# First expert's first weight block: loaded from GpSimd's queue in step 15, split in steps 18 and 19

## The chip, the cores and the metric

The kernel runs on one core of a Trainium2 chip. The metric is the device time of one execution in microseconds (us), as a median over runs. TensorE (PE), VectorE (DVE), ScalarE (ACT), GpSimd (POOL) and SyncE (SP) each work through an instruction stream of their own, in order. SP's stream holds almost only transfers (DMAs); GpSimd can issue transfers as well, on a queue of its own (q0 in the profile; SP's is q1).

## What is computed

Retention attention (4 batches, 8 heads, 768 positions, head size 64, blocks with a decayed state), and behind it a mixture of 8 experts, where each of the 3072 rows goes to the expert with the largest logit:

```python
x = attn_out.transpose(0, 2, 1, 3).reshape(3072, 512)
e_idx = np.argmax(x @ w_gate, axis=1)
for e in range(8):
    mask = e_idx == e
    h = np.maximum(x[mask] @ w1[e], 0.0)          # 512 -> 1024
    out[mask] = gate_w[mask, None] * eom[mask, e, None] * (h @ w2[e])   # 1024 -> 512
```

All in float32. The kernel gets that accuracy from fast products: each factor is split into a high part (a rounded copy) and a low part (the rest), and three products are summed (high by high, low by high, high by low).

## The kernel before

**Stages.** The attention is cut into 24 tiles of 128 rows, n = 0 to 23, six chunks of four batches. A software pipeline runs over steps s = -2 to 21. In step s, `stage_a(s+2)` turns keys and queries of tile s+2 on TensorE (`pk`, `pq`), and ScalarE copies them out (`kT`, `qT`); `stage_c1(s)` multiplies the decayed queries `qd` with the state (into `po`); `stage_b(s+1)` makes the scores (`ps`), which VectorE multiplies with the decay (`at`); `stage_c(s)` adds the scores' part to `po`, ScalarE copies it out as `xT`, and the state is updated from `pst`. Tiles 22 and 23 are finished by straight code behind the loop. GpSimd makes `qd` and `kd` (decayed queries and keys), scatters the routing records of the rows into a table in DRAM (`tab_d`), loads index lists from that table, and gathers rows of x (`xg`). From step 14 on the first expert is known, from the first 12 tiles; in step 15 its first index list is loaded (`load_rows(0, 0, 2, nc.gpsimd)`, called `index_0` below). The second index list is loaded behind the loop, when all earlier scatters have landed (`index_1` below).

**Weights.** Each expert's w1 and w2 come in two pieces of 1 MB each, `raw_i` (128 partitions, four runs of 512 numbers). Three buffers hold them. `load_piece(i)` issues the transfer; `split_hi(i, j)` is a ScalarE cast of a quarter into `whi`; `split_lo2(i, h)` is a VectorE subtraction over half a piece into `wlo` (raw minus `whi`, 128x1024). Before, `load_piece(0)` stood in step 18 (RES + 2, with RES = 16) on SP's queue, pieces 1 and 2 in steps 20 and 21. The four `split_hi(0, ...)` and two `split_lo2(0, ...)` stood behind the loop, between the last tiles. Piece 3 takes the buffer of piece 0 and waits until piece 0 is split.

**What sets the order.** The code stands in the order in which each engine runs it (`tc.manual_schedule()`); waits are added by the framework where an instruction needs another's result or buffer. `work` is a table of what is issued between the parts of a step, by engine GpSimd mostly. The first experts' products (`ph`, then `pyr`) begin as fillers between the last routing steps; behind them TensorE runs through all eight experts.

Of the kernel before, what the change touches and what calls it, by code (L numbers as in the profile page):

```python
# [23 lines left out]
def kernel(  # L24
# [13 lines left out]
    nc = tc.nc  # L38
# [37 lines left out]
    RES = 16  # L76
    RES0 = RES - B
# [23 lines left out]
    def turned_out(i):  # L101
        return pieces[i][1] == 1 and pieces[i][0] in TURNED

    def by_quarter(t):
        return t.rearrange("p (q d c) -> p q d c", q=4, d=4)

    def by_part(t):
        return t.rearrange("p (d q c) -> p q d c", q=4, d=4)

    def load_piece(i, eng=nc.sync, j=None):  # L110
        if i >= len(pieces):
            return
        p, m, s = pieces[i]
        src = (w1, w2)[m][bass.ds(expert[p], 1)]
        src = src[:, :, s * HALF : (s + 1) * HALF] if m == 0 else src[:, s * HALF : (s + 1) * HALF, :]
        if i not in raws:
            raws[i] = wpool.tile([P, 4, 512], F32, tag="raw", bufs=3, name=f"raw_{i}")
        c = slice(0, 4) if j is None else slice(j, j + 1)
        eng.dma_start(raws[i][:, c, :], src.rearrange("e (c p) f -> p (e c) f", p=P)[:, c, :])

    def split_hi(i, j):
        if i >= len(pieces):
            return
        if pieces[i] not in wparts:
            wparts[pieces[i]] = (
                wpool.tile([P, 4, 512], F32R, tag="whi", bufs=4, name=f"whi_{i}"),
                wpool.tile([P, 4, 512], F32R, tag="wlo", bufs=4, name=f"wlo_{i}"),
            )
        src, hi = raws[i][:, j, :], wparts[pieces[i]][0][:, j, :]
        if turned_out(i):  # L130
            src, hi = by_quarter(src), by_part(hi)
        nc.scalar.copy(out=hi, in_=src)  # L132
# [10 lines left out]
    def split_lo2(i, h):  # L143
        sl = slice(2 * h, 2 * h + 2)
        hi, lo = (t[:, sl, :] for t in wparts[pieces[i]])
        nc.vector.tensor_tensor(out=lo, in0=raws[i][:, sl, :], in1=hi.bitcast(F32), op=ALU.subtract)  # L146
# [149 lines left out]
    def blank_rows():  # L296
        norow = wpool.tile([P, E * EB * 3], I32, tag="raw", bufs=3, name="norow")
        nc.gpsimd.memset(norow, NOROW)
        nc.sync.dma_start(tab_d.rearrange("(p r) t -> p (r t)", p=P), norow)
# [132 lines left out]
    def stage_c(n):  # L432
        L = live[n]
        c, b = divmod(n, B)
        vt = qkv[n][2]
        xT = slot(f"xT_{n}")
        for y in range(2):
            po = L["po"][y]
            for m in range(4):
                i, j = divmod(m, 2)  # L440
                nc.tensor.matmul(  # L441
                    po[j * D : (j + 1) * D, i * P : (i + 1) * P],
                    vt[:, 4 * y + m, :],
                    L["at"][y][:, m, :],
                    start=(c == 0),
                    stop=(c == 0 or m >= 2),
                )
            nc.scalar.copy(out=xT[:, 256 * y : 256 * y + 256], in_=po[:, 0:256])
        L["xT"] = xTs[n] = xT
        if c < NCH - 1:  # L450
            pst = bank(f"pst_{n}")
            for m in range(4):
                for y in range(2):
                    nc.tensor.matmul(  # L454
                        pst[y * D : (y + 1) * D, m * D : (m + 1) * D],
                        L["kd"][:, 2 * m + y, :],
                        vt[:, 4 * y + m, :],
                        start=True,
                        stop=True,
                    )  # L460
            psv = pst[:, 0 : 4 * D].rearrange("p (m d) -> p m d", m=4)
            if c == 0:
                nc.vector.tensor_copy(out=state[b], in_=psv)
            else:
                for m in range(4):
                    nc.vector.scalar_tensor_tensor(
                        out=state[b][:, m], in0=state[b][:, m], scalar=qdec[:, m, P - 1 : P], in1=psv[:, m],
                        op0=ALU.mult, op1=ALU.add,
                    )
            weave()  # L470
            weave()
# [356 lines left out]
    def load_rows(p, j0=0, j1=None, eng=nc.sync):  # L828
        if p >= E:
            return  # L830
        n = (KT[p] if j1 is None else j1) - j0
        t = const.tile([32, 4, n, 3], I32, name=f"index_{p}_{j0}")
        src = tab_v[bass.ds(expert[p], 1)][:, :, j0 : j0 + n, :]
        eng.dma_start(t, src.rearrange("e (b r) j t -> (e r) b (j t)", b=4))
        idxs[(p, j0)] = (t, n)
# [381 lines left out]
    with tc.manual_schedule():  # L1217
# [15 lines left out]
        def rec():  # L1233
# [4 lines left out]
            RES0 - 1: ([], [rec], [rec]),  # L1238
            RES0: ([], [], []),
            RES0 + 2: ([], [rec], [rec]),  # L1240
            RES0 + 3: ([], [rec], [rec, lambda: load_rows(0, 0, 2, nc.gpsimd)]),
            RES + 2: ([row(2)], [], [row(3)]),
            RES + 3: ([row(4)], [], [row(5)]),
            RES + 4: ([rec], [], [rec]),
# [4 lines left out]
        for s in range(-2, NTILE - 2):  # L1249
            if s >= 0:  # L1250
                load_up_to(s + AHEAD - (4 <= s <= RES), 2 if s <= RES else 1)
            for i in range(3):
                if s == RES + (2, 4, 5)[i]:
                    load_piece(i)
            if s == -2:
                decay_table()
            if s == 0:
                stage_b(1)
                stage_b2(1)
            rest = stage_a(s + 2)  # L1260
            if late and s != RES + 5:
                late.pop(0)()
            if s >= 1 and s % B == 0:
                logits(s - B, B)
            for f in rest:
                f()
            if s >= 0:
                stage_c1(s)
            stage_a2(s + 2)
            if s == RES + 4:  # L1270
                stage_q(s + 2)
            if s + 1 >= 0 and s != 0:
                stage_b(s + 1)
            if s == RES + 5:
                late.pop(0)()
                seen = rank_counts("plater")
            n = s - 1
            if s >= 1 and s % B == 0:
                logit_rows(s - B)
            if n >= 0 and n % B == B - 1:  # L1280
                choice = route_choose(n + 1 - B, n + 1)
                ranking = route_place(n + 1 - B, n + 1)
                if s != RES + 4:
                    at_once(choice)
                    pace(uncounted[-1][0][0:1, 0, 0:1])
                per_turn[0] = 3 if n >= RES else 2
            if s == RES + 5:
                stage_d2(LAST)
            if s + 1 >= 0 and s != 0:
                stage_b2(s + 1)  # L1290
            stage_k(s + 2)
            if s == RES0 + 2:
                expert_regs(0, order_i, 1)
            if s == RES + 5:
                for f in held[:6]:
                    f()
                x_turn(0, 0)
            gap_work(s, "end")
            if s == RES + 4:
                at_once(choice[:-1])  # L1300
            if 0 <= n < LAST:
                stage_d2(n)
            if s == 0:
                later.extend(inter_tables())
                routing_tables()
                order_tables()
            if s == 1:
                weave(len(later))
            if s == 2:
                blank_rows()  # L1310
            if s >= 0:
                stage_c(s)
            if s == RES + 4:
                choice[-1]()
            if s == RES + 1:
                row_index(0)
                row(0)()
                row(1)()
            if ranking and s == RES + 4:
                late.append(ranking[0])  # L1320
                held = ranking[1:]
                ranking = []
            if ranking and s != RES0:
                late.append(ranking[0])
                later.extend(ranking[1:])
                ranking = []
            if ranking:
                for f in pick_first():
                    f()
                late.append(ranking[0])  # L1330
                later.extend(ranking[1:])
                ranking = []
            if s < RES0 - 2:
                place_scatter(1)

        n = NTILE - 1
        for j in range(2):
            split_hi(0, j)
        stage_c1(n - 1)
        stage_b(n)  # L1340
        stage_b2(n)
# [8 lines left out]
            x_hi(0, g, 0)  # L1350
        for g in range(NPAIR):
            x_lo(0, g, 0)
        split_lo2(0, 0)
        split_hi(0, 2)
        load_piece(3)
        stage_c1(n)
        stage_c(n)
        split_hi(0, 3)
        split_lo2(0, 1)
        for i in range(2):  # L1360
            rows_of(LAST + i)
        logits(LAST, B)
# [249 lines left out]
```

## Time and profile before

| what | value |
|---|---|
| median of three runs | 417.85 us (416.82 to 417.86) |
| the profiled execution, its own time | 415.14 us |
| its span, first to last instruction | 413.4 us |
| TensorE busy | 400.8 us (97%) |
| VectorE, ScalarE, GpSimd busy | 286.7, 190.4, 238.8 us |
| granted TensorE clock, mean | 0.998 |

The span ends with TensorE's last products and the scatter of the last rows. Shares of busy time are means over stages; a stage's own bound is read from what its instructions wait for, and an idle engine matters only where another engine waits for it.

### The profile page before, as it was taken

The numbers are of one execution on the slowest core, as the hardware profiler recorded it, in microseconds if no ns is written. First come the engines' busy times: TensorE is split into PE (matmuls) and PEld (weight loads), VectorE is DVE, ScalarE is ACT, GpSimd is POOL, SyncE is SP. The second block draws the span as 40 slices with busy tenths as digits, with TensorE's granted clock in tenths as the row PEclk, the third lists the DMA queues.
The fourth block names the chain that finished last, engine by engine and source line by source line (L and its number), as shares of the span: only waits on it lengthen the run. The fifth ranks groups of instructions, "written<-read, shape, count | busy, mean of one in ns | idle before, by whom it ended". The sixth has DMA issues, their size and how long they took to land.

```text
span 413.4 us, 10570 instructions
## 1 busy us (share of the span) xinstructions
PE 400.8 (97%) x3869; PEld 367.1 (89%) x3869; DVE 286.7 (69%) x810; ACT 190.4 (46%) x460; POOL 238.8 (58%) x301
## 2 busy tenths in 40 slices
PE   7999999999899999999999999999999999999994
PEld 4889878798698698999999999999999989989983
DVE  2759697877888646876868857957965864873710
ACT  4767665665684033544145325504704543542400
POOL 5367679668846788674783665467386266120012
PEclk9999999999999999999999999999999999999999
DMA  8999898889972764544479548746846884461001
GB/s 177 231 254 246 226 258 224 215 230 259 322 231 79 222 206 144 170 141 135 150 209 297 198 135 241 262 178 200 292 140 186 295 271 151 127 224 46 5 27 52
DMA packets 95103, 79.11 MB, mean 191 GB/s; under 512 B 58445, under 2 KB 70769, under 8 KB 95041
## 3 DMA queue, kind: packets, MB, share of 16 engines
q1 hardware_dynamic: 88080, 64.88, 53.2%
q0 software_dynamic: 6240, 12.93, 10.0%
q8 instruction: 32, 0.52, 0.5%
q10 hardware_dynamic: 720, 0.53, 0.5%
q14 instruction: 31, 0.25, 0.2%
HBM read 62.25 MB, written 16.45 MB: 190 GB/s over the span
## 4 chain that ended last, share of the span: by engine, by line
PE 85%; DVE 6%; DMA 5%; issue 2%; POOL 1%; ACT 0%; POOLq 0%; DVEq 0%; SPq 0%
PE ph_None L86 10%; PE ph_None L87 10%; PE ph_None L85 10%; PE py L87 6%; PE py L86 6%; PE py L85 6%; PE pyr L86 5%; PE pyr L87 5%; PE pyr L85 5%; PE ps L400 4%; PE po L441 4%; PE pk L341 3%; PE po L424 2%; PE pq L341 2%; DVE at L409 2%; PE pst L454 2%
## 5 line engine op out<-in xcount | busy, mean ns | idle before, releaser
L900 POOL DMA_INDIRECT xg<-x_d,rows x100 | 110.6, 1106 | 54.8 <-issue 28.9
L1009 ACT ACTIVATE hhi<-ph_None 128x400 fp32r<-128x400 f32 (+4 forms) x56 | 28.1, 501 | 115.8 <-PE ph_None L87 111.0
L86 PE MATMUL ph_None<-xlo,whi 128*128 128x400 f32 (+4 forms) x224 | 76.2, 340 | 0.0
L87 PE MATMUL ph_None<-xhi,wlo 128*128 128x400 f32 (+4 forms) x224 | 76.1, 340 | 0.0
L85 PE MATMUL ph_None<-xhi,whi 128*128 128x400 f32 (+4 forms) x224 | 76.1, 340 | 0.0
L132 ACT CAST whi<-raw 128x512 fp32r<-128x512 f32 x128 | 74.7, 615 | 2.4 <-DMA raw<-in_moe_w_dram 2.4
L141 DVE TENSOR_TENSOR wlo<-raw,whi 128x512 fp32r<-128x512 f32 x112 | 74.5, 686 | 0.7 <-ACT whi L132 0.5
L1010 DVE SCALAR_TENSOR_TENSOR hlo<-ph_None,hhi 128x400 fp32r<-128x400 f32 (+4 forms) x56 | 31.9, 570 | 35.2 <-ACT hhi L1009 33.2
L87 PE MATMUL py<-hhi,wlo 128*128 128x400 f32 (+2 forms) x128 | 44.4, 347 | 0.0
L86 PE MATMUL py<-hlo,whi 128*128 128x400 f32 (+2 forms) x128 | 44.4, 347 | 0.0
L85 PE MATMUL py<-hhi,whi 128*128 128x400 f32 (+2 forms) x128 | 44.4, 347 | 0.0
L86 PEld LDWEIGHTS ph_None<-xlo,whi 128*128 128x128 f32 x224 | 42.0, 188 | 0.5 <-DVE xlo L935 0.2
L1126 POOL DMA_INDIRECT out_dram<-yn,table x12 | 12.5, 1045 | 51.8 <-DVE yn L1190 34.6
L85 PEld LDWEIGHTS ph_None<-xhi,whi 128*128 128x128 f32 x224 | 42.0, 188 | 0.4
L87 PEld LDWEIGHTS ph_None<-xhi,wlo 128*128 128x128 f32 x224 | 42.0, 188 | 0.2
L345 ACT COPY qT<-pq 64x256 f32<-64x256 f32 x96 | 37.8, 393 | 2.0 <-PE pq L341 1.0
L409 DVE TENSOR_TENSOR at<-ps,decay 128x512 f32<-128x512 f32 x48 | 31.1, 681 | 10.4 <-PE ps L400 10.4
L86 PE MATMUL pyr<-wlo,hhi 128*128 128x512 f32 (+2 forms) x96 | 37.8, 394 | 0.5 <-DVE wlo L146 0.5
L87 PE MATMUL pyr<-whi,hlo 128*128 128x512 f32 (+2 forms) x96 | 37.6, 391 | 0.0
L85 PE MATMUL pyr<-whi,hhi 128*128 128x512 f32 (+2 forms) x96 | 37.5, 390 | 0.0
L931 ACT CAST xhi<-y 128x256 fp32r<-128x256 f32 (+3 forms) x64 | 19.5, 357 | 31.5 <-DVE y L917 31.5
L679 POOL DMA_INDIRECT tab_d<-rec,idx x24 | 26.2, 1090 | 10.0 <-issue 4.1
(216 smaller groups left out, 783.0 us busy)
## 6 DMA issues: line engine op xcount, KB each, us to landing
raw<-in_moe_w_dram SPq DMA_DIRECT2D x32, 1024.0 KB
x_d<-xn SPq DMA_DIRECT2D x22, 256.0 KB
qkv<-in_k_dram SPq DMA_DIRECT2D x40, 128.0 KB
qkv<-in_v_dram SPq DMA_DIRECT2D x20, 256.0 KB
qkv<-in_q_dram SPq DMA_DIRECT2D x36, 128.0 KB
yd<-yo SPq DMA_DIRECT2D x12, 256.0 KB
yr<-yd SPq DMA_DIRECT2D x48, 64.0 KB
xg<-x_d,rows POOLq DMA_INDIRECT x100
```

Of the source, the lines that this page charges most:

```text
L85: nc.tensor.matmul(ps, a[0], b[0], start=first, stop=False)
L86: nc.tensor.matmul(ps, a[0], b[1], start=False, stop=False)
L87: nc.tensor.matmul(ps, a[1], b[0], start=False, stop=last)
L132: nc.scalar.copy(out=hi, in_=src)
L141: eng.tensor_tensor(out=lo, in0=src, in1=hi.bitcast(F32), op=ALU.subtract)
L341: nc.tensor.transpose(out=dst[:, m * P : (m + 1) * P], in_=src[:, m], identity=ident)
L345: copies = [lambda r=r, view=view, src=src: nc.scalar.copy(out=view(qT[r]), in_=src) for r, view, src in query_parts(pq)]
L409: nc.vector.tensor_tensor(out=at, in0=ps.rearrange("p (g t) -> p g t", g=NPAIR), in1=dec[:, j], op=ALU.mult)
L679: nc.gpsimd.indirect_dma_start(out=tab_d, out_offset=bass.IndirectOffsetOnAxis(ap=idx, axis=0), in_=rec, in_offset=None, bounds_check=P * ...
L900: nc.gpsimd.indirect_dma_start(out=xg[(p, i)][:, m * P : (m + 1) * P], out_offset=None, in_=x_q[0 : 4 * rows], in_offset=bass.IndirectOffs ...
L1009: nc.scalar.activation(out=hi[:, r], in_=ph[:, r], func=AF.Relu)
L1010: nc.vector.scalar_tensor_tensor(out=lo[:, r], in0=ph[:, r], scalar=0.0, in1=hi[:, r].bitcast(F32), op0=ALU.max, op1=ALU.subtract,)
```

## The change

The transfer of piece 0 moves from SP's queue in step 18 to GpSimd's queue in step 15, right behind the first index load. The four high splits move into steps 18 and 19, one ahead of and one behind `stage_c` in each; the two low splits move to the end of step 19. No work is added or taken away.

```diff
-            RES0 + 3: ([], [rec], [rec, lambda: load_rows(0, 0, 2, nc.gpsimd)]),
+            RES0 + 3: ([], [rec], [rec, lambda: load_rows(0, 0, 2, nc.gpsimd), lambda: load_piece(0, nc.gpsimd)]),
...
-            for i in range(3):
+            for i in range(1, 3):
                 if s == RES + (2, 4, 5)[i]:
                     load_piece(i)
...
+            if RES + 2 <= s <= RES + 3:
+                split_hi(0, s - RES - 2)
             if s >= 0:
                 stage_c(s)
+            if RES + 2 <= s <= RES + 3:
+                split_hi(0, s - RES)
+            if s == RES + 3:
+                for h in range(2):
+                    split_lo2(0, h)
...
         n = NTILE - 1
-        for j in range(2):
-            split_hi(0, j)
         stage_c1(n - 1)
...
-        split_lo2(0, 0)
-        split_hi(0, 2)
         load_piece(3)
         stage_c1(n)
         stage_c(n)
-        split_hi(0, 3)
-        split_lo2(0, 1)
```

On GpSimd, behind the last scatter of step 15 (names are tiles with the tile number n, then a running number; `rec`, `row0` and `beat` belong to the routing), before:

```order
L834 DMA index_0_0_1829<-tab_d_73 32x4x6
L571 IOTA rec_12_1938 128x4
L572 TENSOR_SCALAR rec_12_1938<-row0_138 128x4
L862 CAST beat_157<-oh_12_1935 1x1
L375 TENSOR_TENSOR qd_18_1912<-qT_18_1877,qdec_132 128x512
```

and with the change:

```order
L834 DMA index_0_0_1829<-tab_d_73 32x4x6
L119 ISA
L119 DMA raw_0_1831<-in_moe_w1_dram 128x4x512
L571 IOTA rec_12_1940 128x4
L572 TENSOR_SCALAR rec_12_1940<-row0_138 128x4
L862 CAST beat_157<-oh_12_1937 1x1
L375 TENSOR_TENSOR qd_18_1914<-qT_18_1879,qdec_132 128x512
```

The transfer now stands between the index load and `qd` of tile 18. On ScalarE, from step 18 to step 20, before:

```order
L345 COPY qT_20_2138<-pq_20_2128 64x256 x4
L448 COPY xT_18_2189<-po_18_0_2144 128x256
L448 COPY xT_18_2189<-po_18_1_2145 128x256
L344 COPY kT_21_2224<-pk_21_2214 128x512
L345 COPY qT_21_2225<-pq_21_2215 64x256 x4
L448 COPY xT_19_2275<-po_19_0_2231 128x256
L448 COPY xT_19_2275<-po_19_1_2232 128x256
L344 COPY kT_22_2311<-pk_22_2301 128x512
```

and with the change:

```order
L345 COPY qT_20_2138<-pq_20_2128 64x256 x4
L132 CAST whi_0_2189<-raw_0_1831 128x512
L448 COPY xT_18_2192<-po_18_0_2144 128x256
L448 COPY xT_18_2192<-po_18_1_2145 128x256
L132 CAST whi_0_2189<-raw_0_1831 128x512
L344 COPY kT_21_2228<-pk_21_2218 128x512
L345 COPY qT_21_2229<-pq_21_2219 64x256 x4
L132 CAST whi_0_2189<-raw_0_1831 128x512
L448 COPY xT_19_2280<-po_19_0_2235 128x256
L448 COPY xT_19_2280<-po_19_1_2236 128x256
L132 CAST whi_0_2189<-raw_0_1831 128x512
L344 COPY kT_22_2319<-pk_22_2309 128x512
```

The four casts stand ahead of copies that TensorE's next steps need, and the first of them waits for the transfer. On VectorE, behind the loop, before:

```order
L935 TENSOR_TENSOR xlo_0_3_2589<-y_0_0_2488,xhi_0_3_2588 128x192
L146 TENSOR_TENSOR wlo_0_2505<-raw_0_2125,whi_0_2504 128x1024 x2
L578 TENSOR_REDUCE mx_20_2667<-pl_20_2636 128x4
L579 TENSOR_TENSOR pl_20_2636<-pl_20_2636,mx_20_2667 128x32
L580 SCALAR_TENSOR_TENSOR pl_20_2636<-pl_20_2636,erev_136 128x32
```

With the change the two L146 stand in step 19, between the state update of tile 19 and the scores of tile 21 (L409 of `at_21`), and L578 follows L935 directly.

## Rows read from the trace of the kernel before

**Rows 1.** Chain that ended last, in order of time: start, us, what.

```profile
124.14 2.65 DMA index<-tab_d
...
132.43 0.50 PE pyr L86
132.92 0.23 PE pyr L87
...
135.76 0.50 PE pyr L86
```

**Rows 2.** Busy time by stretch: length, PE, PEld, DVE, ACT, POOL, clock, DMA, GB/s.

```profile
138.50:400.00 261.50, 261.50 (x1410) 247.84 (x1410) 178.91 (x457) 105.09 (x236) 141.46 (x160) 1.00 0.56 181
```

**Rows 3.** Timeline of PE: start, us, instruction, [idle before, what ended it].

```profile
91.07 0.67 PE L424 MATMUL po<-qd,state 64*64 64x128 f32 x16
...
96.10 1.10 PE L400 MATMUL ps<-qT,kT 64*64 64x128 f32 x32
...
108.04 0.45 PE L424 MATMUL po<-qkv,state 64*64 64x128 f32 x8 [0.32 <-POOL qkv L375]
...
112.38 0.45 PE L424 MATMUL po<-qkv,state 64*64 64x128 f32 x8 [1.53 <-POOL qkv L375]
...
132.43 0.50 PE L86 MATMUL pyr<-wlo,hhi 128*128 128x512 f32 x1 [0.49 <-DVE wlo L146]
```

**Rows 4.** Waits of 130 to 140 us, in total, times, longest.

```profile
PEld pyr L86 <- DVE wlo L146: 1.7, 3, 0.8
```

**Rows 5.** Timeline of POOL.

```profile
2.44 0.96 POOL L215 DMA_DIRECT2D wgs<-in_moe_w_gate_dram  x1 [0.32 <-POOL wgs L214]
...
88.10 0.63 POOL L834 DMA_DIRECT2D index<-tab_d  x1 [3.10 <-DMA tab_d<-rec,idx]
...
89.41 1.27 POOL L375 TENSOR_TENSOR qd<-qT,qdec 128x512 f32<-128x512 f32 x1
...
94.94 1.14 POOL L900 DMA_INDIRECT xg<-x_d,rows  x1 [1.02 <-DVE rec L634]
...
101.34 0.74 POOL L375 TENSOR_TENSOR qd<-qT,qdec 128x256 f32<-128x256 f32 x1
...
105.25 0.75 POOL L375 TENSOR_TENSOR qkv<-qT,qdec 128x256 f32<-128x256 f32 x1
...
115.54 1.97 POOL L679 DMA_INDIRECT tab_d<-rec,idx  x1 [0.30 <-issue]
117.81 0.97 POOL L679 DMA_INDIRECT tab_d<-rec,idx  x1 [0.30 <-issue]
```

**Rows 6.** Timeline of ACT.

```profile
91.23 1.63 ACT L345 COPY qT<-pq 64x256 f32<-64x256 f32 x4
93.25 0.81 ACT L448 COPY xT<-po 128x256 f32<-128x256 f32 x2 [0.38 <-PE po L441]
...
99.36 0.59 ACT L344 COPY kT<-pk 128x512 f32<-128x512 f32 x1 [0.71 <-PE pk L341]
...
110.11 1.14 ACT L132 CAST whi<-raw 128x512 fp32r<-128x512 f32 x2 [2.35 <-DMA raw<-in_moe_w_dram]
```

**Rows 7.** Timeline of DVE.

```profile
102.23 1.29 DVE L409 TENSOR_TENSOR at<-ps,decay 128x512 f32<-128x512 f32 x2 [2.28 <-PE ps L400]
...
114.31 2.36 DVE L146 TENSOR_TENSOR wlo<-raw,whi 128x1024 fp32r<-128x1024 f32 x2
...
126.82 0.16 DVE L869 SCALAR_TENSOR_TENSOR rowf<-index 32x8 f32<-32x8 int32 x1 [0.97 <-DMA index<-tab_d]
```

**Rows 8.** Timeline of SP's queue: start, us to issue, transfer.

```profile
101.14 0.41 SPq L119 DMA_DIRECT2D raw<-in_moe_w_dram  x1
```

**Rows 9.** Transfers of 90.5 to 91.0 us, by queue: packets, MB, share of 16 engines.

```profile
q1 hardware_dynamic: 202, 0.12, 76.5%
...
q0 software_dynamic: 29, 0.00, 5.1%
```

**Rows 10.** Transfers of 105 to 106 us, all queues.

```profile
DMA packets 171, 0.34 MB, mean 341 GB/s; under 512 B 6, under 2 KB 6, under 8 KB 171
```

## Prediction

> **What bounds the kernel now.** I read the chain of waits first, then the busy time by stretch, then each engine's timeline around the moved instructions. From 138.5 to 400 us TensorE is busy for 261.50 of 261.50 us [rows 2], and the change touches nothing there. So only what moves TensorE's work ahead of 138.5 us can count. In the stretch that the change touches, TensorE stands still in three places. Twice, for 0.32 and 1.53 us, it waits for GpSimd's `qd` of tiles 22 and 23 [rows 3]. At 132.43 us it waits 0.49 us for VectorE's low split of piece 2 [rows 3], and weight loads wait there three times, 1.7 us in total [rows 4]. The chain shows what those three cost: at 132.43, at a like row in between and at 135.76 a matmul takes 0.50 where its neighbours take 0.23 [rows 1]. With the idle 0.49 this place loses 0.49 + 3 x 0.27 = 1.3 us. What makes VectorE late there is the index list `index_1`: it lands 2.65 us behind 124.14 [rows 1], and VectorE takes it at 126.82 after 0.97 us of waiting [rows 7].
>
> So the bound ahead of 112 us is GpSimd's stream. It has its last real wait, 1.02 us, at 94.94 [rows 5], and from 97 to 112 us it goes from one instruction to the next. TensorE catches up with it at 108.04 and 112.38. Read forward, this means that TensorE can be late by 0.32 + 1.53 = 1.85 us in steps 18 to 21 and lose nothing, while each delay of GpSimd in there is paid in full.
>
> **The transfer on GpSimd.** An index load takes 0.63 us, and the load of gate weights over 128 partitions and four runs each, the same number of runs as piece 0, 0.96 [rows 5]. I take 0.96; the ends are 0.63 and 1.97, GpSimd's slowest transfer in these rows. It stands ahead of `qd` of tile 18, which ended at 89.41 + 1.27 = 90.68, and TensorE took it at 91.07 [rows 3, 5]. With 0.96 more it is ready at 91.64: TensorE is 0.6 us late, inside the 1.85. GpSimd's own 1.02 us at 94.94 take up the 0.96, so the gathers start when they did, up to 0.1 us. At 1.97 they would start 0.95 late.
>
> **When piece 0 lands.** ScalarE's first cast stands behind `qT` of tile 20, which ends at 91.23 + 1.63 = 92.86 [rows 6]. The issue ends at about 88.73 + 0.96 = 89.7. The index load was issued until 88.73 and has 29 packets moving in 90.5 to 91 [rows 9], some 1.8 us behind; so the first packets of piece 0 move at about 91.5. At 341 GB/s, the rate of a stretch with nearly only large packets [rows 10], 1 MB takes 3.0 us: landed at 94.5, the early end. Q1 uses 76.5% of the engines' time in such a stretch [rows 9], so it will be somewhat slower. The late end comes from piece 0 as it is loaded now: issued until 101.55, landed at 110.11 behind all that q1 held [rows 6, 8], 8.6 us. Counted from the end of the issue these give 98.3, counted from the first packets 100.1. I take 96.0, nearer the early end, because the queue holds nothing else and its packets are large against the key and value loads'. Either way ScalarE waits about 3 us in step 18.
>
> **ScalarE in steps 18 to 20.** Behind the landing it has, until `qT` of tile 22 is out, four casts of about 0.61, two pairs of `xT` (0.81), two `kT` (0.59), two sets of `qT` (1.6) and a small copy, an estimated 0.3: 2.4 + 1.6 + 1.2 + 3.2 + 0.3 = 8.7 us (durations as in [rows 6], and a pair of casts there 1.14). Landing at 96.0 gives `xT` of tile 18 at 97.0, where TensorE, 0.6 late, needs its bank inside the scores at 96.10 + 0.7 = 96.8 [rows 3]; and `qT` of tile 22 at 104.7, where GpSimd takes it at 105.25 [rows 5]. So TensorE gets late by 1 to 2 us in these steps and GpSimd does not. The cover is the 1.85 us; without it the two would be lost.
>
> **Other loads.** The 3.0 us of transfer lie beside q1's loads of keys, queries and values. None is later than the whole 3.0, and TensorE's cover with the next item is 1.85 + 1.3. I take nothing.
>
> **The low splits.** On VectorE they are covered: 2.36 us [rows 7] go into a gap of 2.28 at 102.23 [rows 7], and the scores behind have over 2 us before TensorE needs them. But they run beside GpSimd. Behind the loop a scatter that started while they ran took 1.97 instead of 0.97: 1.00 us lost [rows 5]. In step 19 two of GpSimd's instructions start within 2.4 us of each other (101.34 and the next gather). The ends are nothing and 2.4 us; I take 1.3, next to the row's 1.00, somewhat more because GpSimd has no gap there. This is paid: TensorE's 112.38 becomes 113.7. The Trainium skill has a rule on this (SBUF — State Buffer, Who interferes with whom): a VectorE instruction with two SBUF inputs and a GpSimd instruction that reads SBUF exclude each other, and the later one waits until the first has ended. The scatter's 1.97 agrees with it. Taken strictly, both starts would wait out a split, some 1.6 us in place of 1.3, which leaves the forecast's sign alone and adds 0.3.
>
> **Behind 112 us.** ScalarE's wait of 2.35 us for piece 0 [rows 6] goes; TensorE waited for nothing of ScalarE there, so it brings nothing by itself. The splits leave VectorE's stretch from 114.31 [rows 7], and the scatter at 115.54 gets back its 1.00 us. `index_1` then comes at +1.3 - 1.0 = +0.3 us. VectorE, which follows TensorE in this stretch, is free at 126.82 - 0.97 + 1.3 = 127.15, also +0.3. TensorE arrives 1.3 us later and finds the low splits of piece 2 ready, or nearly: the 1.3 us of waiting are gone. TensorE's own sum is +1.3 - 1.3 = 0; VectorE's chain, where it is still the last, gives +0.3.
>
> **Sum.** +0.3 us. The profiled execution, 415.14 with a span of 413.4, would become 415.4; the median of the runs is 2.7 above it, so 417.85 + 0.3 = 418.1. With the ends of the low splits' term the sum is -0.9 (nothing lost: `index_1` 1.0 earlier, VectorE free 0.1 late, 0.9 of the wait gone) and +1.4 (2.4 lost: VectorE free at 128.25, 1.4 late). A measurement of this kernel can tell about 0.3%, 1.25 us, from no change.
>
> **Rivals.** (1) Slower: the transfer lands too late. It decides where `qT` of tile 22 passes GpSimd's own lateness, at a landing behind 105.25 + 1.3 - 8.7 = 97.8 us. At the late end, 100.1, `qT` is out at 108.8, GpSimd is 3.55 us late from there (what the splits cost lies inside it), and behind 112 us 1.3 (TensorE) or 0.97 (VectorE) come back: 3.55 - 0.97 = +2.6, 420.4. For it: q1 is busy for most of the time; against it: an own queue and large packets. (2) Slower: GpSimd loses the whole 2.4 us to the low splits: +1.4, 419.2. (3) GpSimd isn't hindered: -0.9, 416.9, within 0.3%. For it: its tensor operations have no row beside such a split. (4) Faster: nothing is lost on GpSimd, and with less left on the queues behind 112 us the scatters land a microsecond sooner too (the wait at 88.10 was 3.10 [rows 5]); then all of TensorE's 1.3 us go, and nothing more can: 416.5. (5) The load doesn't come early, because GpSimd holds it back: then ScalarE waits in step 18 as in (1). In the order it stands right behind the index load, so I give it no chance of its own.
>
> **How the numbers follow.** Forecast (+0.3) 0.48, rival 1 0.22, rival 2 0.09, rival 3 0.11, rival 4 0.10. Faster by over 0.3%: 0.10. Slower: rival 1 and most of rival 2, 0.29. Within: 0.61. The range takes in rivals 2, 3 and 4 and most of rival 1: 416.4 to 420.4.
>
> **What would show it.** Right: a cast of piece 0 on ScalarE in step 18 behind a wait of some 3 us for the transfer; TensorE 1 to 2 us late in steps 19 to 21 and its waits for `qd` at 108 and 112 us smaller by that; a gather or `qd` of GpSimd near 102 us that takes up to a microsecond longer; no wait of weight loads for L146 behind 132 us. Wrong: ScalarE's cast without a wait, or with one over 5 us; GpSimd reaching the last `qd` no later than 112.4 us; TensorE's end of the waits near 136 us moved by more than 1.25 us to either side.

## The result, and the profile after

The changed kernel takes **419.05 us** as a median of 11 runs (417.62 to 420.9), the kernel before 416.82 on the same chip (415.13 to 418.28, 11 runs): ratio 1.0066, 95% interval 1.0047 to 1.0085. It is slower by 0.66%, some 2.2 (by the medians) to 2.8 us (by the ratio). The forecast was +0.3 us and "within 0.3%" as the likeliest case; the time lies inside the range, but the kernel is on the slower side. The profiled execution took 419.05, with a span of 417.4. A second measurement (after_again below) gave 1.003 (0.9993 to 1.0066), an interval that just takes in no change, so the size is less certain than the sign.

Behind 138.5 us nothing has changed, as forecast (answers to [rows 2]; length, busy PE, PEld, DVE, ACT, POOL, clock, DMA share, GB/s):

```profile
138.50:400.00 261.50, 261.49 (x1410) 247.41 (x1409) 181.62 (x465) 105.11 (x236) 142.81 (x161) 1.00 0.57 182
```

GpSimd's timeline after (answers to [rows 5]; start, us, instruction, idle time before and what ended it). Everything here comes 3.18 us later than before from the first row on, since `index_0` starts at 91.28 and not at 88.10. Half of that is a longer wait for the scatters ahead of it (4.69 us in place of 3.10), and half is older. Nothing is changed ahead of this place, and unchanged stretches differ that much from execution to execution: in nine profiles of kernels that are alike up to here `index_0` starts between 88.10 and 91.73. So distances are read from `index_0`.

```profile
91.28 0.63 POOL L834 DMA_DIRECT2D index<-tab_d  x1 [4.69 <-DMA tab_d<-rec,idx]
91.90 0.82 POOL L119 DMA_DIRECT2D raw<-in_moe_w_dram  x1
...
93.39 1.26 POOL L375 TENSOR_TENSOR qd<-qT,qdec 128x512 f32<-128x512 f32 x1
...
96.84 1.03 POOL L316 TENSOR_TENSOR kd<-k,kdec 128x512 f32<-128x512 f32 x1
98.90 1.15 POOL L900 DMA_INDIRECT xg<-x_d,rows  x1 [1.03 <-DVE rec L634]
...
104.27 1.83 POOL L900 DMA_INDIRECT xg<-x_d,rows  x1 [0.16 <-issue]
106.13 0.80 POOL L375 TENSOR_TENSOR qd<-qT,qdec 128x256 f32<-128x256 f32 x1
...
116.42 0.74 POOL L375 TENSOR_TENSOR qkv<-qT,qdec 128x256 f32<-128x256 f32 x1
...
126.67 0.64 POOL L834 DMA_DIRECT2D index<-tab_d  x1 [1.46 <-DMA tab_d<-rec,idx]
```

The new transfer's issue costs 0.82 us. From `index_0` to the first gather it is 98.90 - 91.28 = 7.62 us, against 94.94 - 88.10 = 6.84 before: the 0.8 us are paid in full, and the gather's idle time of 1.02 us is still there (1.03 now). A gather that meets the low splits takes 1.83 us where its neighbours take 1.02 or 1.03. VectorE and ScalarE (answers to [rows 7] and [rows 6]):

```profile
95.17 2.72 DVE L869 SCALAR_TENSOR_TENSOR rowf<-index 32x8 f32<-32x8 int32 x1
...
103.85 2.48 DVE L146 TENSOR_TENSOR wlo<-raw,whi 128x1024 fp32r<-128x1024 f32 x2
```

```profile
99.27 0.62 ACT L132 CAST whi<-raw 128x512 fp32r<-128x512 f32 x1 [4.43 <-DMA raw<-in_moe_w_dram]
```

L869, a small instruction that turns the index list into row numbers, takes 2.72 us and ends at 97.89, just where GpSimd's `kd` ends (96.84 + 1.03 = 97.87). Only then can the row numbers be finished that the gather waits for. It was so before, too, where L869 and `kd` both end at 93.9 (VectorE first, then GpSimd):

```profile
93.17 0.78 DVE L869 SCALAR_TENSOR_TENSOR rowf<-index 32x8 f32<-32x8 int32 x1
```

```profile
92.88 1.03 POOL L316 TENSOR_TENSOR kd<-k,kdec 128x512 f32<-128x512 f32 x1
```

ScalarE waits 4.43 us for piece 0. TensorE (answers to [rows 3]):

```profile
94.70 0.67 PE L424 MATMUL po<-qd,state 64*64 64x128 f32 x16 [1.54 <-POOL qd L375]
...
109.83 0.81 PE L341 MATMUL pq<-ident,qkv 128*128 128x128 f32 x4 [1.27 <-DMA qkv<-in_q_dram]
117.21 0.45 PE L424 MATMUL po<-qkv,state 64*64 64x128 f32 x8 [0.86 <-POOL qkv L375]
```

The wait of 1.27 us for a load of queries is new: before, TensorE waited for no key, query or value load in this stretch. SyncE's queue says why (answers to [rows 8]; start, us to issue, transfer). Before, the last pair of query loads was issued at

```profile
98.97 1.32 SPq L178 DMA_DIRECT2D qkv<-in_q_dram  x2
```

which is 10.87 us behind `index_0`; after, it comes 12.76 us behind it, and the pair ahead of it is held up for 4.36 us:

```profile
95.35 4.36 SPq L178 DMA_DIRECT2D qkv<-in_q_dram  x2
...
104.04 1.25 SPq L178 DMA_DIRECT2D qkv<-in_q_dram  x2
```

The transfers of 89 to 100 us by queue (packets, MB, share of 16 engines; answer to [rows 9], over a longer stretch), of before:

```profile
DMA packets 7579, 2.84 MB, mean 259 GB/s; under 512 B 6793, under 2 KB 7307, under 8 KB 7576
...
q1 hardware_dynamic: 7488, 2.69, 95.5%
q0 software_dynamic: 88, 0.12, 3.3%
```

and of after:

```profile
DMA packets 5173, 2.85 MB, mean 259 GB/s; under 512 B 4338, under 2 KB 4783, under 8 KB 5172
...
q1 hardware_dynamic: 4864, 1.78, 68.0%
q0 software_dynamic: 308, 1.05, 29.4%
```

This pair is the main reading of the case. The DMA engines were full before (95.5 + 3.3%) and are full after, and they move as much: 2.84 and 2.85 MB. The megabyte on GpSimd's queue does not come beside the key, query and value loads but in their place; q1 moves 2.69 MB before and 1.78 after. The picture stays if the stretch is moved along with `index_0`: from 92.18 to 103.18 us after, q1 moves 1.53 MB of 2.74, at a DMA share of 0.94. In small_load below, where the transfer has only 16 KB, q1 moves 2.62 MB in 89 to 100 us.

### The profile page after: what moved, and what is told of

Same layout as the page of the kernel before. It is cut to its first block, busy times and chain, and to the rows that moved or that the text cites. A ratio compares the mean times of both kernels' runs of the same rounds, so it can differ in the third digit from the quotient of the medians.

```text
span 417.4 us, 10573 instructions
## 1 busy us (share of the span) xinstructions
PE 400.0 (96%) x3869; PEld 366.4 (88%) x3869; DVE 288.9 (69%) x810; ACT 190.5 (46%) x460; POOL 239.7 (57%) x302
## 4 chain that ended last, share of the span: by engine, by line
PE 81%; DVE 10%; DMA 5%; SPq 1%; issue 1%; POOL 1%; ACT 0%; POOLq 0%; DVEq 0%
PE ph_None L85 10%; PE ph_None L86 10%; PE ph_None L87 10%; PE py L86 6%; PE py L87 6%; PE py L85 6%; PE pyr L86 5%; PE pyr L87 5%; PE pyr L85 5%; DVE at L409 3%; PE ps L400 3%; DMA qkv<-in_q_dram 2%; PE po L441 2%; PE ph L85 2%; PE ph L86 2%; PE ph L87 2%
## 5 line engine op out<-in xcount | busy, mean ns | idle before, releaser
L900 POOL DMA_INDIRECT xg<-x_d,rows x100 | 112.6, 1126 | 56.3 <-issue 29.5
L409 DVE TENSOR_TENSOR at<-ps,decay 128x512 f32<-128x512 f32 x48 | 31.1, 680 | 11.3 <-PE ps L400 11.3
```

The source lines that it names most:

```text
L409: nc.vector.tensor_tensor(out=at, in0=ps.rearrange("p (g t) -> p g t", g=NPAIR), in1=dec[:, j], op=ALU.mult)
L900: nc.gpsimd.indirect_dma_start(out=xg[(p, i)][:, m * P : (m + 1) * P], out_offset=None, in_=x_q[0 : 4 * rows], in_offset=bass.IndirectOffs ...
```

## The experiments

Theory A put the price on GpSimd's stream: the issue, and the low splits that hold up a gather. Theory B put it on the megabyte that takes the place of q1's loads. Distances in one profile each, in us, beside the ratio of the times to the kernel before on the same chip:

| kernel | `index_0` to last `qd` | to `chosen` | last query loads issued | ratio (95%) |
|---|---|---|---|---|
| before | 23.48 | 33.15 | 10.87 | 1 |
| the change | 25.14 | 34.78 | 12.76 | 1.0066 (1.0047-1.0085) |
| the change, again | 26.06 | 35.70 | 13.95 | 1.003 (0.9993-1.0066) |
| small_load | 24.33 | 33.98 | 9.42 | 1.0009 (0.9974-1.0043) |
| load_only | 24.38 | 36.60 | 15.52 | 1.0049 (1.0018-1.008) |
| low_back | 26.30 | 38.13 | 16.54 | 1.0046 (1.0011-1.0082) |
| extra_load | 24.30 | 35.28 | 13.79 | 1.0054 (1.0023-1.0085) |
| load_on_sp | 24.31 | 33.98 | 10.33 | 1.0075 (1.0039-1.0111) |
| after_one_input | 25.18 | 34.83 | 13.31 | 1.0026 (0.9997-1.0056) |
| before_one_input | 23.47 | 33.14 | 11.20 | 0.9997 (0.9961-1.0032) |

`qd` is GpSimd's last (for tile 23), and `chosen` is TensorE's first product behind the last waits (L968, 121.25 in the kernel before); the fourth column is also counted from `index_0`. From `chosen` to the end it is 291.2 to 292.2 us in all ten, 292.15 before. Each row of distances is a single execution, which can lie 2 us off the median of its kernel: that of load_only took 421.34 us (median 419.12), that of extra_load 417.59 (419.5). The distances show which waits occur; the size of a price is read from the ratio.

**after_again**: the changed kernel as it is, on the chip of the next three.

> The changed kernel once more, for a second profile of it. Between the two profiles at hand TensorE is already 2.0 us later in step 17, ahead of anything that was changed, and GpSimd's wait for the scatters ahead of the first index load is 4.69 instead of 3.10 us. Theory A (the price is paid on GpSimd's stream: 0.8 us of issue that delays qd and kd of tiles 18 and 19, and with them VectorE's index rows, and 0.8 us of a gather that waits for a low split): both prices are in this profile too, the index rows (L869) above 2 us, one gather near 1.8 us, whatever the wait for the scatters is. Theory B (the transfer slows the loads of keys and queries, and ScalarE waits for it): ScalarE's wait in step 18 is again 4 to 5 us, and TensorE waits over 1 us for queries of tile 22 or 23. Ratio to the kernel before 1.005 to 1.008 by both.

418.62 us; the ratio, 1.003, lies below the expected 1.005 to 1.008. In its profile the low splits meet two of GpSimd's instructions and not one: a `qd` of 1.70 us (0.75 beside it) and a gather of 1.83, 0.95 + 0.81 = 1.8 us, where the first profile shows 0.80 + 0.06 = 0.86. TensorE stands 0.57 us for query loads, not the "over 1 us" of theory B. By the profile it also stands twice for VectorE, 1.01 us behind the row numbers (L874) and 1.06 behind the low splits, which took 3.25 us here:

```profile
108.41 0.68 PE L341 MATMUL pq<-ident,qkv 128*128 128x128 f32 x4 [1.06 <-DVE oh L584]
```

GpSimd's last `qd` comes 2.58 us later than before and `chosen` 2.55: in both profiles of the change the path to `chosen` is GpSimd's.

**small_load**: the issue without the megabyte.

```diff
+            t = const.tile([P, 4, 8], F32, name="small_raw")
+            src = w1[bass.ds(expert[0], 1)][:, :, 0:8]
+            nc.gpsimd.dma_start(t, src.rearrange("e (c p) f -> p (e c) f", p=P))
...
+            RES0 + 3: ([], [rec], [rec, lambda: load_rows(0, 0, 2, nc.gpsimd), small_load]),
```

> The kernel before, with one more transfer on GpSimd behind the first index load: 512 runs as in the weight load, but of 32 bytes (16 KB in all), into a tile that nobody reads. It has GpSimd's time of issue without the 1 MB. Theory A: GpSimd spends 0.8 to 1.0 us on it, VectorE's index rows (L869) take 0.8 us or more longer, the gathers start 0.8 to 1.0 us later against the index load, and the kernel is 0.8 to 1.0 us slower (ratio 1.002). Had the 1.02 us that GpSimd waits at the first gather taken it up, as the prediction said, it would cost at most 0.1 us. Theory B: 0.

417.75 us: 0.09%, not to be told from nothing, and as little from the 0.2% of theory A, since the interval reaches from -0.26 to +0.43%. The time does not decide here; the profile shows where the issue goes. It takes 0.82 us for 16 KB as for 1 MB, and is paid on GpSimd (24.33 - 23.48 = 0.85). TensorE waits for no load, only for `qd`; its last wait is as long as before, 0.83 us later from `index_0`:

```profile
114.44 0.45 PE L424 MATMUL po<-qkv,state 64*64 64x128 f32 x8 [1.53 <-POOL qkv L375]
```

**load_only**: the transfer as in the change, all splits where they were before (the diff is against the changed kernel and shows the first of the splits).

```diff
             RES0 + 3: ([], [rec], [rec, lambda: load_rows(0, 0, 2, nc.gpsimd), lambda: load_piece(0, nc.gpsimd)]),
...
-            if RES + 2 <= s <= RES + 3:
-                split_hi(0, s - RES - 2)
...
+        for j in range(2):
+            split_hi(0, j)
```

> Only the transfer moves to GpSimd in step 15; all splits stay behind the loop. Theory A: 0.8 us of issue on GpSimd passes on to the gathers in full, nothing is given back: +0.8 us (ratio 1.002), TensorE's wait for qd of tile 23 near 2.3 us instead of 1.53. Theory B: TensorE waits for keys or queries in steps 20 and 21 by up to 2 us, but ScalarE waits for nothing in step 18 or behind the loop; GpSimd's cover takes most of it: 0 to +1 us, and the wait for qd of tile 23 is smaller than 1.53.

419.12 us: a price as large as the change's is there with no split moved, more than either theory expected (0.8 and 0 to 1 us). In its profile GpSimd is 0.9 us late, the issue's part, but `chosen` is 3.45 us late, since TensorE itself waits for keys (and 1.1 us for ScalarE behind the loop):

```profile
100.65 0.63 PE L341 MATMUL pk<-ident,k 128*128 128x128 f32 x4 [2.77 <-DMA k<-in_k_dram]
110.57 0.63 PE L341 MATMUL pk<-ident,qkv 128*128 128x128 f32 x4 [0.64 <-DMA qkv<-in_k_dram]
```

**low_back**: the change with only the low splits put back behind the loop (against the changed kernel).

```diff
-            if s == RES + 3:
-                for h in range(2):
-                    split_lo2(0, h)
...
+        split_lo2(0, 0)
         load_piece(3)
         stage_c1(n)
         stage_c(n)
+        split_lo2(0, 1)
```

> The changed kernel with the two low splits back behind the loop; the transfer and the high splits stay early. Theory A: no gather takes more than 1.2 us in step 19 to 20, GpSimd's stream gets 0.8 to 0.9 us back there; a scatter behind the loop loses up to 1.0 us again and the waits of weight loads for low splits near 132 us return in part: within 0.5 us of the changed kernel (ratio to before 1.004 to 1.007). Theory B: nothing changes for the transfer and ScalarE; the same ratio.

419.02 us. The gathers of steps 19 and 20 take 1.02 or 1.03 us, so the splits' part is gone, and the time is no shorter. TensorE waits for loads instead, and is so late that GpSimd's last two `qkv` wait 1.43 and 0.57 us for ScalarE's `qT`:

```profile
95.67 1.09 PE L441 MATMUL po<-at,v 128*64 128x128 f32 x16 [1.80 <-DMA v<-in_v_dram]
99.35 0.63 PE L341 MATMUL pk<-ident,k 128*128 128x128 f32 x4 [2.12 <-DMA k<-in_k_dram]
```

**extra_load and extra_two**: the kernel before, with one or two pieces loaded once more than needed in step 15 (the second line is the edit of extra_two).

```diff
-            RES0 + 3: ([], [rec], [rec, lambda: load_rows(0, 0, 2, nc.gpsimd)]),
+            RES0 + 3: ([], [rec], [rec, lambda: load_rows(0, 0, 2, nc.gpsimd), lambda: load_piece(0, nc.gpsimd), lambda: load_piece(1, nc.gpsimd)]),
```

> The kernel before with one transfer more: piece 0 is loaded once on GpSimd's queue in step 15, as in the change, and again on SyncE's in step 18; the splits stay behind the loop. It differs from small_load only in the size, 1 MB in place of 16 KB. Theory A (only the issue on GpSimd counts): as small_load, 417.7 us, TensorE waits for no key, query or value load between 94 and 112 us. Theory B, in a sharper form (the 16 DMA engines are full from 89 to 113 us, share 0.93 to 1.05 in the kernel before, so a megabyte more at some 255 GB/s puts every later key, query and value load back by about 4 us): 418.9 to 419.6 us, TensorE waits at least 1 us for such loads, and SyncE issues the last pair of query loads at least 3 us later than the 98.97 of before.

> The kernel before with two transfers more on GpSimd's queue in step 15, pieces 0 and 1 (2 MB), both loaded again on SyncE's queue as before; the splits stay behind the loop. It doubles the dose of extra_load. Theory B (the DMA engines are full, each megabyte more puts the key, query and value loads back by about 4 us): the last pair of query loads is issued some 8 us later than before's 98.97, TensorE waits 4 us or more for such loads, and the price is about twice extra_load's 0.5%: ratio 1.008 to 1.013. Theory A (only the issues on GpSimd count, 0.82 us each): ratio 1.002 to 1.004.

extra_load took 419.5 us against 416.88, ratio 1.0054; extra_two 429.31 against 424.98, ratio 1.0111 (1.0078 to 1.0144). (The chip of extra_two runs the kernel before in 425 us, so only ratios are compared.) 16 KB, 1 MB and 2 MB cost 0.09, 0.54 and 1.11%. The intervals of the first two overlap, but extra_two's lower end, 0.78%, lies above the 0.4% that two issues would cost by theory A: the price goes with the bytes, not with the issues alone. The transfers of 89 to 100 us in extra_load and in extra_two:

```profile
q1 hardware_dynamic: 4903, 1.82, 66.3%
q0 software_dynamic: 336, 1.12, 30.6%
```

```profile
q0 software_dynamic: 466, 1.71, 49.6%
q1 hardware_dynamic: 3041, 1.31, 43.3%
```

q1 falls from 2.69 MB to 1.82 and 1.31. TensorE's waits, extra_load first:

```profile
97.40 0.63 PE L341 MATMUL pk<-ident,k 128*128 128x128 f32 x4 [1.90 <-DMA k<-in_k_dram]
```

```profile
99.16 0.44 PE L341 MATMUL pq<-ident,q 128*128 128x128 f32 x2 [0.48 <-DMA q<-in_q_dram]
...
103.78 1.09 PE L441 MATMUL po<-at,v 128*64 128x128 f32 x16 [1.91 <-DMA v<-in_v_dram]
```

In extra_load the last query loads are issued at 102.83, 3.9 us later than before (3 or more expected), of which 2.9 lie behind `index_0`. In extra_two the listed waits for loads are 2.4 us, less than the 4 expected.

**load_on_sp**: the change, with the early transfer on SyncE's queue.

```diff
-lambda: load_piece(0, nc.gpsimd)]),
+lambda: load_piece(0)]),
```

> The change, but the transfer of piece 0 is issued by SyncE in the same place of step 15; the splits stay early. Theory A: GpSimd gets its 0.82 us back, from index_0 to the first gather it takes 6.8 us as before, and about 0.8 us of the time come back: 418.2. Theory B: the megabyte still stands ahead of the key, query and value loads, now in their own queue: 419 us or more, TensorE waits at least 1 us for them and the last pair of query loads is issued behind 102 us, though index_0 to the first gather is back at 6.8.

420.16 us, the highest ratio of the kernels with one megabyte. `index_0` to the first gather is back at 6.82 us, so GpSimd's issue is gone, and nothing is won. SyncE runs ahead and issues the megabyte at 84.74 us, so it stands ahead of more loads, and the routing records that GpSimd scatters land later too:

```profile
95.50 1.09 PE L341 MATMUL pk<-ident,k 128*128 128x128 f32 x4 [4.24 <-DMA k<-in_k_dram]
```

```profile
94.54 0.63 POOL L834 DMA_DIRECT2D index<-tab_d  x1 [7.93 <-DMA tab_d<-rec,idx]
```

Its loss lies ahead of `index_0`, at 94.54 later than in any other of these profiles, which is why its distances in the table look harmless. Part of its price may be the clock's (last section).

**before_one_input and after_one_input**: L869 with one SBUF operand.

```diff
-        nc.vector.scalar_tensor_tensor(
-            out=gf, in0=t[:, :, :, 2], scalar=float(4 * NT), in1=t[:, :, :, 2], op0=ALU.is_lt, op1=ALU.mult
+        nc.vector.tensor_scalar(
+            out=gf, in0=t[:, :, :, 2], scalar1=NOROW - 1, scalar2=None, op0=ALU.bitwise_and
```

> The kernel before with one edit: the index rows' small VectorE instruction (L869) reads one SBUF operand (a bitwise and) in place of two. Theory A says that L869 waits for GpSimd's kd, and GpSimd's gather then for VectorE: so L869 takes under 0.2 us in place of 0.78, the gather's 1.02 us of idle time shrink to 0.4 or less, everything behind on GpSimd comes 0.6 us earlier, TensorE's wait for the last qd falls from 1.53 to about 0.9, and the time is 0.5 us below the kernel before (ratio 0.9985). If the circle of waits is not there, nothing moves.

> The changed kernel with the same edit of L869. Theory A: L869 falls from over 2 us to under 0.2, the first gather starts directly behind kd of tile 19, index_0 to the first gather is 6.6 us in place of 7.6, and about 1 us comes back against the changed kernel where GpSimd is the bound: 418.0. Theory B: the loads of keys and queries set the time in steps 19 to 23, so the gather comes earlier and the time stays within 0.4 us of the changed kernel's 418.6 to 419.0.

417.61 us (0.9997) and 417.96 (1.0026, not clearly different from the change's 1.003 and 1.0066). The expectation failed: L869 still takes 1.59 and 2.58 us and still ends with `kd`, and the first gather starts 6.84 and 7.62 us behind `index_0` as without the edit. In before_one_input, VectorE and GpSimd:

```profile
95.97 1.59 DVE L869 TENSOR_SCALAR rowf<-index 32x8 int32<-32x8 int32 x1 [0.17 <-DMA index<-tab_d]
```

```profile
96.50 1.03 POOL L316 TENSOR_TENSOR kd<-k,kdec 128x512 f32<-128x512 f32 x1
```

**before_index_psum**: the same edit, and the result goes to PSUM.

```diff
-        gf = const.tile([32, 4, n], F32, name=f"rowf_{p}_{j0}")
+        if (p, j0) == (0, 0):
+            gf = prs[-1].take([P, 4, n], I32)[0:32]
```

> The kernel before with one edit: the index rows' instruction L869 reads one SBUF operand and writes to PSUM instead of SBUF, and L874 reads it there. The run with one SBUF operand but an SBUF result still took 1.59 us and still ended with GpSimd's kd, so the number of inputs alone is not what makes it wait. Theory P (an SBUF-to-SBUF VectorE instruction can wait for GpSimd's, one with PSUM at one end does not): L869 takes under 0.25 us and ends ahead of kd of tile 19, the gather's idle time falls from 1.02 us to 0.5 or less, and the time is 0 to 0.7 us below the kernel before. If L869 still ends with kd, whatever its operands, theory P falls and the tie of GpSimd and VectorE has another reason.

425.89 us against 425.68 (1.0006, 0.998 to 1.0031). The instruction (now L874) takes 0.17 us in the middle of `kd`, VectorE first, then GpSimd:

```profile
95.56 0.17 DVE L874 TENSOR_SCALAR pr<-index 32x8 int32<-32x8 int32 x1
```

```profile
94.75 1.03 POOL L316 TENSOR_TENSOR kd<-k,kdec 128x512 f32<-128x512 f32 x1
96.71 1.14 POOL L905 DMA_INDIRECT xg<-x_d,rows  x1 [0.93 <-DVE rec L636]
```

So the tie is cut by the place of the result, in this one profile. But VectorE came to it only at 95.56 here, so the gather's idle time fell to 0.93 and not to 0.5, and no time was won. The same edit on the changed kernel was not run.

**before_wide and after_wide** were to take load off the DMA engines, by reading keys and values in longer runs.

> The kernel before with lighter transfers: keys and values of tiles 16 to 23 are read as one contiguous run per partition (1 or 2 KB) in place of runs of 256 bytes. The bytes are as many, but they land in another order, so the attention of these tiles is another one than the reference's; the work of every engine stays. Base for after_wide. The DMA share of 80 to 100 us falls from 0.86 and 1.00 to 0.7 or less. Both theories: TensorE did not wait for these loads before, so the time stays within 0.3% of the kernel before.

> The changed kernel with the same lighter transfers of keys and values (another order, so another attention for tiles 16 to 23). Theory B: the DMA engines have room for piece 0, it lands within 5 us of its issue, TensorE waits for no key, query or value load, and the price of the change against before_wide falls to the 0.8 us of the issue and the 0.9 to 1.8 us of the low splits, less the 1 us that comes back behind the loop: within 0.3% of before_wide. Theory A: the price was GpSimd's and does not depend on the transfers: still 0.4 to 0.7% over before_wide.

They settle nothing. With another attention more rows go to single experts than their lists hold, and a further loop works these off at the end; the times, 482.4 to 487.5 us and 482.4 to 493.2, lie over one another. The DMA share of 80 to 110 us fell only to 0.78, 0.84 and 0.94 in before_wide (0.86, 1.00 and 1.00 before), and with the change was 0.70, 0.92 and 1.00 again; TensorE waited 0.8 us for queries.

## Where the prediction was right and where wrong, step by step

The time lies in the range and on the slower side, as forecast. But the price is 1.4 to 2.2 us and not 0.3, and it was not reached as forecast: the range holds it because rivals had made it wide that did not occur, which is luck. Three terms failed: the other loads, taken at nothing; GpSimd's idle time, taken as slack; and the 1.3 us that were to come back behind 112 us.

**"Other loads: I take nothing"** failed, and the experiments bear most on it. It held that no load would be late by more than the 3.0 us of the transfer, and that TensorE had cover of 1.85 + 1.3 us for it. What misled was a half-microsecond window [rows 9] in which q1 held 76.5%, read as room; over 89 to 100 us the engines are full. There the megabyte takes an estimated 4 us at the stretch's 259 GB/s, and the last query loads come 1.9 to 5.7 us later in the kernels with a megabyte early on GpSimd's queue. TensorE's waits of 1.9 to 3.9 us for loads (extra_load, load_only, low_back) are over the 1.85 us. That one early megabyte with its issue is enough for such a price, with no split moved, is shown by extra_load and load_only. In the changed kernel itself the listed waits for loads are 1.27 and 0.57 us, inside the cover, so there this term does not set `chosen`; GpSimd does.

**The transfer on GpSimd.** The issue's size was near (0.96 forecast, 0.82 measured). That GpSimd's 1.02 us of idle time take it up was wrong. The idle time ends with VectorE's row numbers, and VectorE's L869 ends with GpSimd's last `kd`; push GpSimd back and its wait moves along. The wait was read as slack without asking what its releaser itself waits for. Worth 0.8 us on GpSimd, and 0.83 at `chosen` in small_load; whether that much reaches the time, its interval cannot tell. The Trainium skill (SBUF — State Buffer, Who interferes with whom) names a second case beside the two SBUF inputs of the prediction: `tensor_scalar`, which can run in a mode that takes both ports when its operands meet certain conditions. The three forms of L869 beside GpSimd's tensor operations agree with it: 0.78 to 2.72 us with two inputs, 1.59 and 2.58 with one, 0.17 with the result in PSUM.

**When piece 0 lands.** Right: forecast 96.0 with `index_0` at 88.10; measured 99.27 - 3.18 = 96.1, and 96.8 in the second profile, ahead of the 97.8 from which rival 1 decided. ScalarE's wait was 4.4 to 4.9 us in place of 3, which matters to nobody: GpSimd didn't wait for `qT` in either profile of the change. From the end of its issue the megabyte took 6.4 to 8.3 us. The Trainium skill (DMA: Bandwidth & Descriptors, Anatomy of one DMA — SWDGE (gpsimd) path) has a fit that gives an estimated 4.4 us; beside a full q1 the runs show about half as much again or more.

**The low splits.** Forecast 1.3 us with ends 0 and 2.4; measured 0.86 and 1.8. Right within its bounds, and right that it is paid on GpSimd. That VectorE has it covered held in the first profile; in the second TensorE waits 1.06 us behind it, inside its cover. And low_back takes the splits away and wins nothing that can be measured (1.0046 against 1.003): in its profile TensorE waits 3.9 us for loads.

**Behind 112 us.** The forecast gave 1.3 us back there, from a stall at 132.43 [rows 3, 4]. That stall does not come with the order of the kernel before each time. small_load and before_one_input keep all splits behind the loop, and have no idle TensorE there; their weight loads wait 0.8 us in total, twice, as in the changed kernel, where [rows 4] shows 1.7, three times (small_load, 128 to 142 us):

```profile
PEld pyr L86 <- DVE wlo L146: 0.8, 2, 0.4
```

From `chosen` to the end both take 291.2 us, the changed kernel 291.3 and 292.1. So what was forecast to come back stood in the one profile that was read, and not in two others of that order. GpSimd's scatter did get its microsecond back: with the change none behind the loop takes over 1.13 us, while one takes 1.97 in small_load, too. It reaches no later time.

**The sum.** GpSimd's part, with the terms as measured, is 0.82 + 0.86 = 1.7 us or 0.82 + 1.8 = 2.6, in place of 0 + 1.3; the two profiles show 1.66 and 2.58 at the last `qd`, and 1.63 and 2.55 at `chosen`. The return of 1.0 to 1.3 us is not there. That agrees with the 1.4 to 2.2 us of the two measurements. Under this lies the second limit, the loads, with a like price: take away the splits' part (low_back) or the issue on GpSimd (load_on_sp), and the price does not shrink; the one kernel without the early megabyte, small_load, has none that is clear of noise. Rival 1 had the right sign, by a landing that was too late, and that was not the way; rival 2's time, 419.2, was hit, by other terms. What stays open is how the price divides between the two in a median run, since profiles of one kernel differ by 1 us, and what the clock adds (last section).

## What to carry to other kernels

Before a transfer is moved earlier, read the DMA share over several microseconds of the stretch it is moved into. Here it was 1.00 over 89 to 100 us, and the bytes were paid by the loads behind, whether the transfer stood on GpSimd's queue or on SyncE's. Idle time is slack only if what ends it does not itself hang on the waiting engine. A stall that is to be won back should be seen in more than one profile of the same order.

## What was not expected of the hardware

A small VectorE instruction of 32x8 numbers, 0.17 us long, took 0.78 to 2.72 us and ended with the last of a chain of GpSimd operations, across the borders between them: they stand back to back, and as a rule of these profiles it did not get in between. In extra_two it did, at the border behind the first `kd` (94.77 + 1.03 = 95.80), and the next instruction, which takes 0.69 us elsewhere, paid instead:

```profile
95.64 0.18 DVE L869 SCALAR_TENSOR_TENSOR rowf<-index 32x8 f32<-32x8 int32 x1 [0.69 <-DMA index<-tab_d]
95.86 2.54 DVE L874 TENSOR_SCALAR rows<-rowf 32x8 int32<-32x8 f32 x4
```

A two-input VectorE instruction with one operand in PSUM ran beside the same chain in 0.16 us (L655, at 94.90 in the changed kernel).

GpSimd's issue of a transfer of 512 runs takes 0.82 us for 16 KB and for 1 MB.

TensorE's granted clock may have taken part. Behind load_on_sp's wait of 4.24 us it fell to the lower of its two levels, 0.50 in this stretch:

```profile
95.50:96.50 1.00, 1.00 (x5) 1.00 (x6) 0.00 (x0) 0.00 (x0) 0.94 (x3) 0.50 1.00 260
```

Over its runs the mean granted clock was 0.990, against 0.995 of the kernel before on that chip, an estimated 418 x 0.005 = 2 us of its price. For the changed kernel it was 0.9925 in the first measurement and 0.9948 in the second, where the ratio was smaller, too; the kernel before had 0.9948 beside the second, and beside the first it is not on record. From 0.995 to 0.9925 is an estimated 418 x 0.0025 = 1.0 us. In load_only, low_back and extra_load the clock was 0.9957, 0.9943 and 0.9941, against 0.9948 and 0.9947 of the kernel before, so their prices are not the clock's.
